# Four weight loads issued on ScalarE's queue, ahead of its table load, in a linear-attention and MLP block

## The chip, the cores and the metric

The kernel runs on one NeuronCore of a Trainium2 chip. The metric is the device time of one execution in microseconds, as the median of the runs; the median of a changed kernel is compared with the median of the kernel before. A profile (one execution recorded by the hardware profiler) gives the rest: its times count from the start of its span.

In the profile's rows PE is TensorE (PEld its weight loads), DVE is VectorE, ACT is ScalarE, POOL is GpSimd, and SP is SyncE, which only issues DMAs. A "q" behind an engine means its sequencer. `L361` is line 361 of the kernel.

## The reference

A block of two parallel branches over 2048 tokens of width 512, all in float32: a layer norm without weights, a linear attention of 32 heads with 16 columns each, and a two-layer MLP with a squared ReLU and 1376 hidden columns.

```python
def reference(A_x, A_wqkv, A_wo, B_x, B_w1, B_b1, B_w2, B_b2):
    def _A_ref(x, wqkv, wo):
        B, S, D = x.shape
        H = 32; Dh = D // H
        qkv = (lambda x, *d: x.transpose(*d))((x @ wqkv).reshape(B, S, 3, H, Dh), 2, 0, 3, 1, 4)
        q, k, v = qkv[0], qkv[1], qkv[2]
        phi = lambda t: jnp.where(t > 0, t + 1, jnp.exp(t)) + 1e-6
        pq, pk = phi(q), phi(k)
        kv = jnp.einsum("bhsd,bhse->bhde", pk, v)
        z = jnp.einsum("bhsd->bhd", pk)
        num = jnp.einsum("bhqd,bhde->bhqe", pq, kv)
        den = jnp.einsum("bhqd,bhd->bhq", pq, z)[..., None] + 1e-6
        o = num / den
        return (lambda x, *d: x.transpose(*d))(o, 0, 2, 1, 3).reshape(B, S, D) @ wo
...
    x = A_x
    xn = _layernorm(x, axis=-1)
    return x + _A_ref(xn, A_wqkv, A_wo) + _B_ref(xn, B_w1, B_b1, B_w2, B_b2)
```

## The kernel before

The 2048 tokens are 16 tiles of 128 rows (`NT = 16`, `P = 128`). A float32 product is made from float32r parts: each operand is split into a high part and the rest, and three of the four partial products are added in PSUM (`wk[0]`, `wk[1]` are the high and low part of the key weights, `xsb` those of the transposed tokens). The kernel first runs over the 16 token tiles for the keys and the sums that linear attention needs (`kx`), then over queries, attention and the MLP. The order of instructions on each engine is the order in which the code writes them (`manual_schedule`); the framework adds the semaphore waits.

What matters here is the start, before the first product.

- ScalarE loads its function table in the first lines of the kernel (L68); its first ACTIVATE is the logarithm for tile 0's inverse root (L225).
- TensorE runs 11 matmuls on zeros (L472), which appear as 22 rows in the profile, while the first data comes.
- SyncE issues, one after the other on its queue: token tile 0 and token tile 1 (`x0`, 256 KB each, `load_x`, L156), the four chunks of the key columns of `wqkv` (`rk`, `load_k`, L479: 128 rows of 2 KB each, cut out of rows of 6 KB), token tiles 2 and 3 in one load (`x2`, 512 KB, L156), and, behind a wait for a small copy on GpSimd (L540), token tiles 4 to 7 (`x4`, 1 MB). Only SyncE issues DMAs in the whole kernel.
- VectorE takes the statistics of tile 0, then of tile 1 (L214 and L215; each waits for its tile's load). Then come three short steps that refine the inverse root of tile 0 (L234 to L236), its normalisation (`xp`, L253), and the same for tile 1.
- ScalarE, behind the logarithm and exponential of tile 0 and of tile 1 (L225, L226), copies the high part of key chunk 0 (`wkh<-rk`, L109, in `heads_k`), then the transposed tokens of tile 0 (`xs1h`, L316), then chunk 1, and so on; chunks 2 and 3 come later.
- TensorE transposes tile 0 (`pt`, L300) when it is normalised, and begins the key products (`pk`, L361) with the first half of tile 0 and key chunk 0.

Of the kernel before, what the change touches and what calls it, by code (L numbers as in the profile page):

```python
# [18 lines left out]
def kernel(  # L19
# [29 lines left out]
    nc = tc.nc  # L49
    xf = x.rearrange("b s d -> (b s) d")  # L50
    of = out.rearrange("b s d -> (b s) d")
    S, D = xf.shape
# [11 lines left out]
    FP = NF * P  # L64
    FL = F - (NF - 1) * P
    assert D == 512 and S % BT == 0 and FL % 32 == 0 and FL < P

    nc.scalar.preload_act_table_set("natural_log_exp_and_others")  # L68

    keep = ctx.enter_context(tc.tile_pool(name="keep", bufs=1))  # L70
    work = ctx.enter_context(tc.tile_pool(name="work", bufs=1))
# [12 lines left out]
    def next_tag(of):  # L84
        k, n = turns[of]
        turns[of][0] = (k + 1) % n
        return f"{of}{k}"

    def two(name):
        return keep.tile([P, 2, 512], F32, name=name, tag=next_tag("x"))  # L90

    def four(name, tag, dt=F32, pool=None):
        return (pool or work).tile([P, TB, 512], dt, name=name, tag=tag)
# [60 lines left out]
    def load_x(i, t):  # L154
        n = t.shape[1]
        nc.sync.dma_start(t, xf[i * P:(i + n) * P, :].rearrange("(i p) d -> p i d", i=n))  # L156
        for k in range(n):
            xr[i + k] = t[:, k]
# [6 lines left out]
    def chunk(w, j, a, b):  # L165

        return w[j * P:(j + 1) * P, a:b]
# [306 lines left out]
    t, rk = two("x0"), four("rk", "r0")  # L474
    for i in range(2):
        load_x(i, t[:, i:i + 1])
    def load_k(*js):
        for j in js:
            nc.sync.dma_start(rk[:, j], chunk(wqkv, j, D, 2 * D))  # L479

    load_k(*range(NJ))
    load_x(2, two("x2"))
    nc.gpsimd.memset(ident, 0.0)
    nc.gpsimd.affine_select(out=ident, in_=ident, compare_op=OP.not_equal, fill=1.0, base=0,
# [629 lines left out]
```

## Time and profile before

| | |
|---|---|
| median of 3 runs | 422.36 us (422.19 to 422.56) |
| the profiled execution | 422.49 us, of which the span is 420.8 us |
| PE busy | 415.2 us (99%) |
| PE weight loads busy | 343.6 us (82%) |
| DVE / ACT / POOL busy | 294.2 / 254.0 / 27.6 us |
| granted TensorE clock | 1.00 |
| DMA | 46.16 MB, mean 110 GB/s |
| first transpose on PE (L300) | starts at 6.46 us |

A row of the timeline gives the start, the length, the engine, the line and the operation, and in brackets how long the engine was idle before it and what ended that. The chain of waits is followed back from the last instruction to what released each step; it tells which work set the end. A row of the stages gives a window and its length, then for each engine its busy time and the number of its instructions, and last the granted clock, the mean share of the 16 DMA engines that is busy, and GB/s. A DMA row ends with the time from issue to landing.

### The profile page before, as it was taken

How to read it: one execution, taken by the hardware profiler on the slowest of the kernel's cores; microseconds unless marked ns; L12 is line 12 of the kernel's file. 1: busy time of each engine (PE TensorE's matmuls, PEld its weight loads, DVE VectorE, ACT ScalarE, POOL GpSimd, SP SyncE). 2: the span in 40 equal slices, each digit the busy share in tenths (PEclk: the TensorE clock that was granted, in tenths of full speed). 3: DMA queues.
4: the chain of work that ended last, by engine and by line, in shares of the span. 5: the costliest groups of instructions: out<-in, count | busy, mean ns of one | idle time of the engine just before them, and what ended most of it. 6: DMA issues, size and time to landing. Idle time of an engine off the chain costs nothing.

```text
span 420.8 us, 5373 instructions
## 1 busy us (share of the span) xinstructions
PE 415.2 (99%) x1860; PEld 343.6 (82%) x1860; DVE 294.2 (70%) x536; ACT 254.0 (60%) x451; POOL 27.6 (7%) x50
## 2 busy tenths in 40 slices
PE   7999999999999999999999999999999999999996
PEld 7788888888887888888888888888888888888885
DVE  6886767777578877677579475586967667577343
ACT  5867777675467767665457362676667665546230
POOL 3242222220000000000000000000000000000000
PEclk9999999999999999999999999999999999999999
DMA  7885422800412231645026652401120654024502
GB/s 240 286 243 157 130 89 92 278 15 3 112 50 77 75 100 26 199 82 169 0 85 191 173 196 97 124 0 50 51 75 25 202 101 149 2 95 97 152 0 100
DMA packets 44818, 46.16 MB, mean 110 GB/s; under 512 B 5716, under 2 KB 31060, under 8 KB 44536
## 3 DMA queue, kind: packets, MB, share of 16 engines
q1 hardware_dynamic: 44792, 45.84, 36.5%
q8 instruction: 14, 0.23, 0.2%
q14 instruction: 12, 0.10, 0.1%
HBM read 32.71 MB, written 8.91 MB: 99 GB/s over the span
## 4 chain that ended last, share of the span: by engine, by line
PE 98%; DVE 1%; DMA 1%; ACT 0%; issue 0%
PE acc L128 39%; PE b L453 23%; PE kx L380 10%; PE pk L361 10%; PE pq L361 10%; PE pz L128 1%; PE b L128 1%; PE pkv L773 1%; PE pm L128 1%; DMA x<-in_A_x_dram 1%; PE pt L300 1%; PE end L128 0%; DVE st L214 0%; DVE xp L253 0%; DVE res L903 0%; ACT xs1h L316 0%
## 5 line engine op out<-in xcount | busy, mean ns | idle before, releaser
L128 PE MATMUL acc<-w2r,s 128*128 128x512 f32 x498 | 116.6, 389 | 0.0
L128 PEld LDWEIGHTS acc<-w2r,s 128*128 128x128 f32 x498 | 93.5, 188 | 19.6
L453 PE MATMUL b<-T,aop 128*128 128x512 f32 x240 | 59.6, 389 | 0.0
L453 PEld LDWEIGHTS b<-T,aop 128*128 128x128 f32 x240 | 45.0, 188 | 9.4
L380 PE MATMUL kx<-pk,tok 128*128 128x512 f32 x192 | 46.8, 392 | 0.0
L380 PEld LDWEIGHTS kx<-pk,tok 128*128 128x128 f32 x192 | 35.6, 188 | 7.9 <-DVE pk L369 0.6
L128 PE MATMUL acc<-mh,aTsr 128*128 128x512 f32 x96 | 30.3, 390 | 0.0
L109 ACT ACTIVATE w2r<-r 128x512 fp32r<-128x512 f32 x32 | 20.0, 625 | 13.8 <-PE acc L128 11.3
L120 DVE TENSOR_TENSOR w2r<-r,w2r 128x512 fp32r<-128x512 f32 x32 | 21.9, 685 | 7.3 <-ACT w2r L109 7.2
L453 PE MATMUL b<-xs0h,aop 128*128 128x512 f32 x80 | 26.4, 391 | 0.0
L117 POOL TENSOR_TENSOR tok<-xp,tok 128x512 fp32r<-128x512 f32 x16 | 21.7, 1362 | 54.9 <-ACT tok L109 54.9
L117 DVE TENSOR_TENSOR s<-c,s 128x512 fp32r<-128x512 f32 x20 | 13.8, 692 | 16.3 <-ACT s L109 16.3
L356 DVE SCALAR_TENSOR_TENSOR q<-pq,q 128x512 f32<-128x512 f32 x16 | 11.0, 689 | 14.9 <-ACT q L354 14.9
L109 ACT ACTIVATE aop<-S 128x512 fp32r<-128x512 f32 x20 | 12.6, 629 | 14.6 <-DVE S L702 9.4
L128 PEld LDWEIGHTS acc<-mh,aTsr 128*128 128x128 f32 x96 | 18.0, 188 | 3.8
L903 DVE TENSOR_TENSOR res<-acc,res 128x512 f32<-128x512 f32 x16 | 11.0, 692 | 14.2 <-PE acc L128 14.2
L352 ACT ACTIVATE q<-pq 128x512 f32<-128x512 f32 x16 | 9.4, 591 | 18.5 <-PE pq L361 18.5
L199 POOL MEMSET r<- 32x512 f32 x3 | 1.6, 522 | 278.2 <-DVE w2r L120 272.3
L128 PE MATMUL acc<-ml,aTsr 128*128 128x512 f32 x48 | 18.7, 390 | 0.0
L453 PEld LDWEIGHTS b<-xs0h,aop 128*128 128x128 f32 x80 | 15.0, 188 | 3.4 <-ACT rz L441 0.3
L453 PE MATMUL b<-xs0l,aop 128*128 128x512 f32 x40 | 15.6, 389 | 0.0
L285 DVE STREAM_TRANSPOSE at<-g 128x512 f32<-128x512 f32 x16 | 10.5, 689 | 6.8 <-DMA g<-q 6.8
(192 smaller groups left out, 826.7 us busy)
## 6 DMA issues: line engine op xcount, KB each, us to landing
r<-in_B_w_dram SPq DMA_DIRECT2D x49, 256.0 KB, 3.2
res<-in_A_x_dram SPq DMA_DIRECT2D x8, 512.0 KB, 5.9
g<-q SPq DMA_DIRECT2D x64, 64.0 KB, 2.1
out_dram<-res SPq DMA_DIRECT2D x15, 256.0 KB, 2.1
x<-in_A_x_dram SPq DMA_DIRECT2D x5, 512.0 KB, 5.6
via<-xp SPq DMA_DIRECT2D x5, 512.0 KB, 2.6
xg<-via SPq DMA_DIRECT2D x20, 128.0 KB, 3.0
xTd<-t SPq DMA_DIRECT2D x8, 256.0 KB, 3.1
```

The costliest lines, as they stand in the source:

```text
L109: nc.scalar.activation(o, i, AF.Copy, bias=bias)
L117: ENG[el].tensor_tensor(out=l, in0=src, in1=f32(h), op=OP.subtract)
L120: nc.vector.tensor_tensor(out=l, in0=src, in1=f32(h), op=OP.subtract)
L128: nc.tensor.matmul(ps, lhsT=a[u], rhs=b[v], start=first and n == 0, stop=last and n == 2)
L285: nc.vector.transpose(o.rearrange("p j (r t) -> p r j t", r=NJ), G.rearrange("p r (j c) -> p r j c", j=NJ))
L300: nc.tensor.transpose(t[k][:, at:at + P], xp[i][:, j * P:(j + 1) * P], ident)
L352: nc.scalar.activation(p, ps, AF.Relu, scale=-1.0)
L356: nc.vector.scalar_tensor_tensor(p, ps, 0.0, p, op0=OP.max, op1=OP.add)
L361: nc.tensor.matmul(ps, lhsT=cols(i)[u][:, j, slot(i)], rhs=w[v][:, j, :], start=first and n == 0, stop=last and n == len(steps) - 1)
L380: nc.tensor.matmul(kxp[c], lhsT=tok[i][:, u, c * P:(c + 1) * P], rhs=pk[i][:, v], start=i == 0 and (u, v) == first, stop=i == NT - 1 and ( ...
L453: nc.tensor.matmul(ps, lhsT=a[u][:, j * P:(j + 1) * P], rhs=b[v][:, j, :], start=first and j == 0 and n == 0, stop=last and j == 1 and n == 2,
L903: nc.vector.tensor_tensor(out=r[:, a:z], in0=ps, in1=r[:, a:z], op=OP.add)
```

## The change

The table load moves from the head of the kernel to behind the four loads of the key chunks, and these four are issued by ScalarE in place of SyncE. On ScalarE the order is then: four DMA issues, the table load, and all else as before. On SyncE it is: tile 0, tile 1, tiles 2 and 3, and all else as before. The instructions of the other engines and their order are the same. As two lines fall away and one comes in, a line of the kernel after stands one or two numbers lower than in the kernel before (L214 becomes L212, L484 becomes L483).

```diff
@@ -65,8 +65,6 @@
     FL = F - (NF - 1) * P
     assert D == 512 and S % BT == 0 and FL % 32 == 0 and FL < P
 
-    nc.scalar.preload_act_table_set("natural_log_exp_and_others")
-
     keep = ctx.enter_context(tc.tile_pool(name="keep", bufs=1))
     work = ctx.enter_context(tc.tile_pool(name="work", bufs=1))
     small = ctx.enter_context(tc.tile_pool(name="small", bufs=4))
@@ -476,9 +474,10 @@
         load_x(i, t[:, i:i + 1])
     def load_k(*js):
         for j in js:
-            nc.sync.dma_start(rk[:, j], chunk(wqkv, j, D, 2 * D))
+            nc.scalar.dma_start(rk[:, j], chunk(wqkv, j, D, 2 * D))
 
     load_k(*range(NJ))
+    nc.scalar.preload_act_table_set("natural_log_exp_and_others")
     load_x(2, two("x2"))
     nc.gpsimd.memset(ident, 0.0)
     nc.gpsimd.affine_select(out=ident, in_=ident, compare_op=OP.not_equal, fill=1.0, base=0,
```

## The prediction

> **What bounds the kernel now.** I read the chain of waits first, over the first 30 us. Its columns are start, length (us) and what held the end.
>
> ```profile
> 0.82 2.76 DMA x<-in_A_x_dram
> ...
> 3.60 0.71 DVE st L214
> ...
> 4.51 0.59 DVE st L214
> ...
> 5.77 0.55 DVE xp L253
> ...
> 6.46 0.42 PE pt L300 x2
> ...
> 6.91 0.39 ACT xs1h L316
> ...
> 7.35 0.50 PE pk L361
> 7.85 0.44 PE pt L300 x4
> 8.28 4.34 PE pk L361 x19
> ```
>
> The reader is to see that the chain enters TensorE at 6.46 and never leaves it again: 19 matmuls in 4.34 us are 0.228 us each, and line 4 of the page gives PE 98% of the whole span. So nothing after about 8 us can be gained or hidden; what moves the first transpose (L300) moves the end by as much. Ahead of it stands one DMA, the load of token tile 0, and then VectorE's own order: statistics of tile 0, statistics of tile 1, and only then the normalisation of tile 0 (L234 to L253). So tile 1's landing is on this path too, as soon as it comes after VectorE is ready for it.
>
> The timeline (start, length, engine, line, operation) gives the issues and who is ready when.
>
> ```profile
> 0.81 1.28 ACT L68 ACT_TABLE_LOAD   x1 [0.81 <-PEq L1100]
> 0.82 0.86 SPq L156 DMA_DIRECT2D x<-in_A_x_dram  x2
> ...
> 1.72 1.85 SPq L479 DMA_DIRECT2D rk<-in_A_wqkv_dram  x4
> ...
> 3.62 4.23 SPq L156 DMA_DIRECT2D x<-in_A_x_dram  x2
> ...
> 4.43 0.66 DVE L214 BATCH_NORM_STATS2 st<-x 128x6 f32<-128x512 f32 x1
> 4.55 0.29 ACT L225 ACTIVATE y<-mv,eps 128x1 f32<-128x1 f32 x1 [2.45 <-DVE mv L215]
> ```
>
> Tile 1's statistics start at 4.43 with no wait in brackets: x1 had landed, by how much earlier this view doesn't say. The table load ends at 2.09, 2.46 us before ScalarE's first ACTIVATE.
>
> Then the transfers: issue to landing of the key chunks one by one (last number), and the DMA engines by stage (last three columns: clock, DMA share, GB/s).
>
> ```profile
> rk<-in_A_wqkv_dram SPq DMA_DIRECT2D x1, 256.0 KB, 4.1
> ...
> rk<-in_A_wqkv_dram SPq DMA_DIRECT2D x1, 256.0 KB, 4.3
> ```
>
> ```profile
> 1.85:2.50 0.65, 0.65 (x5) 0.65 (x5) 0.00 (x0) 0.24 (x1) 0.52 (x4) 1.00 0.94 189
> 2.50:3.10 0.60, 0.60 (x4) 0.60 (x4) 0.00 (x0) 0.00 (x0) 0.04 (x1) 1.00 0.99 328
> 3.10:3.60 0.50, 0.50 (x5) 0.50 (x4) 0.00 (x1) 0.00 (x0) 0.00 (x0) 1.00 1.06 397
> 3.60:4.20 0.60, 0.60 (x5) 0.60 (x5) 0.60 (x1) 0.00 (x0) 0.00 (x0) 1.00 0.91 242
> 4.20:4.80 0.60, 0.60 (x5) 0.60 (x5) 0.56 (x3) 0.25 (x1) 0.00 (x0) 1.00 0.66 249
> 4.80:5.40 0.60, 0.55 (x5) 0.35 (x4) 0.53 (x4) 0.30 (x3) 0.00 (x0) 1.00 1.13 318
> 5.40:6.00 0.60, 0.00 (x0) 0.00 (x0) 0.53 (x3) 0.57 (x3) 0.00 (x0) 1.00 0.99 341
> ```
>
> From 1.85 to 3.6 the 16 DMA engines are full (0.94 to 1.06) while they carry x0 and x1 alone. Length times GB/s adds up to 123, 320, 518, 663, 812, 1003 and 1208 thousand bytes at the ends of these rows. One 256 KB load is 262 thousand: x0 has moved at 2.92, x0 and x1 together at 3.62, a third load at 4.69, a fourth at 5.53. x0 landed at 3.58, 0.66 after its bytes. The key chunks 0 and 1, third and fourth, landed at 1.72 + 4.1 = 5.82 and about 2.19 + 4.3 = 6.49 (issues 0.47 apart).
>
> **The change part by part.** *Table load behind four issues.* ScalarE now starts with four DMA issues. On SyncE the same four take 1.85 us together; so the table load runs from about 2.66 to 3.95, still 0.60 before the 4.55 at which ScalarE is first wanted: cost 0. Bounds: an issue may cost between 0.43 and the longest single issue near here, 1.20 (the one of L652). From 0.61 each the cover by tile 0's load and statistics is gone and every microsecond counts; but if tile 1 is late, as below, VectorE first wants y0 behind tile 1's statistics, and the issues may then take about 1.0 each. I take 0.43.
>
> *SyncE without the four.* It is free 1.90 us sooner, so x2 (512 KB) is issued at about 1.72 instead of 3.62. The load of x4 behind it waits for GpSimd's copy (L540, at 7.26), which waits for tile 1's normalisation constants, so it moves with the path; the stores and loads behind it follow. x2 landed at about 9.1 and its statistics begin at 9.52 behind other VectorE work: sooner is worth 0.
>
> *Key chunks sooner.* wkh of chunk 0 (5.81) stands on ScalarE behind the roots of tile 1, done at 5.87 by the timeline's rows, so its landing at 5.82 held nothing: 0 gained. At most the three wider gaps between matmul starts from 6.8 to 8.4 (0.53, 0.34, 0.31 instead of 0.23) could shrink, 0.5 us in all, and the rows put these to the transposes and to xs1h, not to the keys. Chunks 2 and 3 are wanted at 8.91; x2 and they together end where the same 2.1 MB ended before, about 9.1, and with the path 1.4 later that is hidden by 1.2 us. Without that delay it would cost 0.2.
>
> *Token tiles share the engines.* This is the term that counts. Before, x0 and x1 had full engines for themselves. Now rk0 starts at 0.81 on ScalarE's queue beside x0 at 0.82, and rk1 beside x1. If the engines serve both queues evenly, x0 ends with 524 thousand bytes moved and x1 with 1049 thousand, twice as far down. Ends for x1's landing: at the best rate of the rows (397 GB/s) from 1.85 with the ramp of the first row (0.65 us for 123 thousand), 2.50 + 926/397 = 4.83, plus x0's 0.66 = 5.49; or as rk1 did with as many bytes ahead, 6.49. I take 5.8, under the middle, since the idle third of the engines in 4.20 to 4.80 (0.34 x 0.6 = 0.2 us) gets work sooner. Tile 1's statistics then start 0.02 behind the landing, at 5.82 instead of 4.43: +1.4. x0's own delay (landing about 4.3 instead of 3.58) is inside that: its statistics end before x1 comes. From there every row up to 6.46 follows in its old order, and TensorE passes all of it on.
>
> The Trainium skill, page "DMA: Bandwidth & Descriptors", section "Issuing engines are not separate DMA queues", speaks against this change: DMAs issued from the scalar and sync engines run on the same 16 engines and interleave, and a second issuer saves only issue time. The full DMA share beside x0 agrees; by this rule the sum is a loss, not a gain.
>
> *Sum:* 0 + 0 + 0 + 1.4. The profiled execution took 422.49 (span 420.8 and 1.7 around it) and would take 423.9, with a span of 422.2. It is 0.13 above the median of 422.36; against that median the sum is 422.36 + 1.4 = **423.8**.
>
> **The rivals.** *B, whole loads in turn:* each engine serves one queue's share of a whole load, then the other's: x0, rk0, x1, rk1. Then x1 is the third, landing between 4.69 (bytes alone) and 5.82 (as rk0 did); 4.69 + 0.66 = 5.35 is +0.94: 423.3. For it: x0's share on one engine is only 262/16 = 16 thousand bytes. Against it: ScalarE may be first, and then x1 is fourth again. The same page, section "Queues, rings and completion order", says that an engine drains a packet of some 9 to 17 descriptors from one row before it turns to the next; nothing in this trace has two busy load queues, so no row agrees or disagrees.
>
> *C, not slower:* the mechanism is a head start of SyncE's loads, its place the DMA engines' queues at 1.85. If x0 and x1 are served before the keys (ScalarE's queue starts later, or is served behind), x1 lands before 4.43 and nothing changes: 422.4. It decides when ScalarE's first bytes come over about 1 us after SyncE's. Against it: both issuers are released within 0.01 us.
>
> *D, faster:* the gaps of 0.5 us from 6.8 to 8.4 and the ramp of the first row (189 GB/s against 397, 0.3 us) both vanish because two queues fill the engines sooner: -0.8, 421.5. Against it: the share is 0.94 already in the ramp.
>
> *E, clock drop:* between the warm-up matmuls (end 5.34) and L300 (6.46) TensorE idles 1.12; with +1.4 it is 2.5. The warm-up starts 18 matmuls in its first 3.77 us, 0.21 each, and 6 rows lie in its last 0.72, 0.12 each: the same work at half and at full pace. If the idle stretch brings the slow pace back for as long, half of 3.77 is lost: +1.9, 425.7. The Trainium skill, "TensorE: Matmul & The Clock Gate", Part 1, has the clock fall only after an idle window of about 3.4 us; by it 2.5 is safe, and no run here shows where the limit lies.
>
> *F, the table load ends last:* with issues of 1.20 each on ScalarE it ends at 0.81 + 4.8 + 1.28 = 6.89; the roots of tile 0 then end 0.5 later, at 7.4, against the 6.7 at which VectorE would want them: +0.7 more, 424.5.
>
> **How the numbers follow.** The likeliest case 0.50, B 0.20, C 0.14, D 0.04, E 0.06, F 0.06. I call no change what lies within 0.2%, 0.84 us, about what a measurement here can tell from none. Slower: 0.50, E and F 0.12, and 0.11 of B (its low end is below +0.84): 0.73. Same: C and the rest of B, 0.23. Faster: 0.04. Range: the likeliest's own is 423.4 to 424.5 (5.49 and 6.49); down to C's 422.3, up to 424.9 so that part of E stays out.
>
> **What would show it.** After: x1's landing at 5.5 to 6.5, an idle DVE before the second L212 (its L214) put to DMA x, the first transpose at about 7.9, the matmuls behind it at 0.228 as before, a table load that ends near 3.95. B shows as x1 near 5.3. C would show the second statistics still at 4.43, and the sum fails. E would show matmuls at 0.4 us start to start behind the transposes; F an idle DVE put to ACT y.

## The result, and the profile after

The changed kernel takes 425.18 us (median of 6 executions, 424.83 to 426.15), the kernel before 422.52 beside it (422.19 to 422.76). The ratio is 1.0066, with a 95% interval of 1.0053 to 1.0079: 2.7 us slower. The profiled execution is the longest of the six, 426.15 with a span of 424.4, 3.6 us more than the span before.

The chain of waits after (start, length, what held the end):

```profile
1.26 4.18 DMA x<-in_A_x_dram
...
5.46 0.70 DVE st L212
...
7.54 0.67 PE pt L298 x2
...
8.67 0.79 PE pk L359
9.46 0.85 PE pt L298 x4
10.31 5.94 PE pk L359 x19
```

The DMA at the head is now the second token tile's, issued at 1.26. The second statistics start at 5.46 instead of 4.43, 1.03 late, and the first transposes at 7.54 instead of 6.46, 1.08 late. Then the same work takes longer on TensorE itself: from the first transpose to the 19 matmuls 10.31 - 7.54 = 2.77 instead of 1.82, and the 19 matmuls 5.94 instead of 4.34, 0.313 each on average instead of 0.228. 1.08 + 0.95 + 1.60 = 3.63, the whole difference of the two spans.

The start in the timeline (the length of a row that joins several issues runs from the first to the end of the last, so the 8.56 of SyncE's row is mostly waiting), and the loads one by one with their time to landing:

```profile
0.81 1.87 ACTq L477 DMA_DIRECT2D rk<-in_A_wqkv_dram  x4
...
0.81 8.56 SPq L154 DMA_DIRECT2D x<-in_A_x_dram  x4
...
2.71 1.28 ACT L480 ACT_TABLE_LOAD   x1 [2.71 <-issue]
4.48 0.69 DVE L212 BATCH_NORM_STATS2 st<-x 128x6 f32<-128x512 f32 x1 [3.54 <-DMA x<-in_A_x_dram]
...
5.46 0.69 DVE L212 BATCH_NORM_STATS2 st<-x 128x6 f32<-128x512 f32 x1
```

```profile
rk<-in_A_wqkv_dram ACTq DMA_DIRECT2D x1, 256.0 KB, 3.8
...
rk<-in_A_wqkv_dram ACTq DMA_DIRECT2D x1, 256.0 KB, 4.6
x<-in_A_x_dram SPq DMA_DIRECT2D x1, 256.0 KB, 4.2
```

Key chunk 0 lands at 0.81 + 3.8 = 4.6, and tile 0 just before 4.48; tile 1 at 1.26 + 4.2 = 5.5, key chunk 1 at about 1.25 + 4.6 = 5.85. The loads come in pairs, one of each queue. The table load ends at 2.71 + 1.28 = 3.99, well before ScalarE's first ACTIVATE at 5.42.

The granted clock is the share of full speed at which TensorE is let run. Here are stretches of 3.41 us, which is how long the half-speed stretches on record last (window, length, PE busy and the number of matmuls that lie in it wholly or in part, clock, DMA share, GB/s):

```profile
3.33:6.74 3.41, 2.56 (x12) 1.00 1.01 377
6.74:10.16 3.42, 2.58 (x10) 1.00 0.32 120
10.16:13.57 3.41, 3.41 (x10) 1.00 0.79 302
13.57:16.90 3.33, 3.33 (x18) 1.00 0.62 157
```

A stretch that is full of matmuls holds 10 of them up to 13.57, and 18 behind it. The clock column says 1.00 throughout, because the trace has no clock record before the first grant of full speed; the pace tells that TensorE ran at half speed until 13.57. (The mean granted clock of this execution, 0.999, comes from the last 1.3 us of the span, behind the last matmul, where the clock is 0.50.) The other five executions have a mean granted clock of 0.996 over spans of 423.1 to 423.5: 0.004 x 423.4 / 0.5 = 3.4 us at half speed, which by this estimate costs 1.7. With the 1.03 by which the second statistics are late that is 2.7, the median's loss.

### The profile page after: what moved, and what is told of

Read it like the earlier page. It is cut to its first block, busy times and chain, and to the rows that moved or that the text cites. A ratio compares the mean times of both kernels' runs of the same rounds, so it can differ in the third digit from the quotient of the medians.

```text
span 424.4 us, 5374 instructions
## 1 busy us (share of the span) xinstructions
PE 418.6 (99%) x1860; PEld 346.1 (82%) x1860; DVE 294.5 (69%) x536; ACT 253.9 (60%) x451; POOL 27.6 (7%) x50
## 4 chain that ended last, share of the span: by engine, by line
PE 97%; DMA 1%; DVE 1%; issue 0%; ACT 0%; SPq 0%
PE acc L126 38%; PE b L451 22%; PE pk L359 11%; PE kx L378 10%; PE pq L359 10%; PE pz L126 1%; PE b L126 1%; DMA x<-in_A_x_dram 1%; PE pkv L772 1%; PE pt L298 1%; PE pm L126 1%; PE end L126 0%; DVE st L212 0%; DVE xp L251 0%; DVE res L902 0%
```

## The experiments

Each was timed beside the kernel before, which took 422.48 to 422.56. Lines of the kernels stand within two or so of those above.

**The kernel after with a longer warm-up.**

```diff
-    WARM = 11
+    WARM = 16
```

> The kernel after, with 16 warm-up matmuls (32 rows) instead of 11 (22 rows), so that TensorE has work until about 7 us. Theory 1: of the +2.7 us, 1.0 is tile 1's late landing (second statistics at 5.46 instead of 4.43) and the rest a slow TensorE clock that follows the longer idle stretch ahead of the first transpose; without that stretch the time is 422.5 + 1.0 = 423.5, and no matmul behind the first transposes is 0.4 us after the one before. Theory 2: the rest is late data further on (key chunks, tiles 2 and 3, later loads); then more warm-up work changes nothing and the time stays at 425.2.

423.75, ratio 1.0033 (1.0022 to 1.0045). The second statistics are as late as in the kernel after, at 5.54, but the loss is 1.2 instead of 2.7. In its profile TensorE's stretches are:

```profile
2.17:5.58 3.41, 3.41 (x18) 1.00 0.97 347
5.58:8.99 3.41, 2.46 (x19) 1.00 0.70 260
```

and in its timeline the first transposes start at

```profile
7.62 0.63 PE L298 MATMUL pt<-ident,xp 128*128 128x128 f32 x4 [0.70 <-DVE y L232]
```

The first stretch is full of warm-up rows, the next is still busy for 2.46, and behind it the matmuls follow at 0.23. The first transposes are 1.16 late (7.62 instead of 6.46), and that is about the whole of the 1.2. Theory 1 holds, theory 2 falls: no data further on was late.

**The kernel before with the longer warm-up** (the same edit).

> The kernel before, with 16 warm-up matmuls instead of 11. Control: both theories expect 422.5, if the added 10 rows end before the first transpose is ready at 6.46 us; at the slow pace of 0.21 us a row all 32 would end at 7.7 and cost up to 1.2, at the fast pace from 4.6 on they end at 6.2 and cost nothing.

422.76, ratio 1.0007 (0.9998 to 1.0016): no difference that the interval can tell. By itself the longer warm-up makes the kernel no faster, and by the interval at most 0.7 slower.

**The delay without the transfers.** In the kernel before, between the two statistics:

```diff
-    two_tiles = statistics(0), statistics(1)
+    two_tiles = [statistics(0)]
+    for _ in range(2):
+        nc.vector.tensor_scalar(zb, xr[0], two_tiles[0][2][:, 0, 0:1], two_tiles[0][2][:, 0, 1:2], op0=OP.subtract, op1=OP.mult)
+    two_tiles.append(statistics(1))
```

> The kernel before, its transfers unchanged, with two more VectorE instructions of the normalisation's form (0.55 us each) between the statistics of tile 0 and of tile 1; their result is overwritten later and not used. The first transpose is thereby 1.1 us late, with no change to any DMA. Theory 1: a late start of any cause lets the clock fall: 422.5 + 1.1 + 1.7 = 425.3. Theory 2 (the rest of the loss comes from the DMAs): 422.5 + 1.1 = 423.6, and the matmuls keep the fast pace.

425.29, ratio 1.0056 (1.0038 to 1.0073): nearly the whole loss of the kernel after, with every DMA as before. The executions lie at 423.8 (two of six, granted clock 1.00), 425.2 to 425.4 (three, 0.995 to 0.996) and 426.5 (one, 0.991). The profiled one is one of the first kind:

```profile
2.99:6.40 3.41, 2.90 (x14) 1.00 0.92 293
6.40:9.81 3.41, 1.99 (x12) 1.00 0.67 242
```

```profile
7.57 0.63 PE L300 MATMUL pt<-ident,xp 128*128 128x128 f32 x4 [1.68 <-DVE y L234]
```

The first transposes are 1.11 late here, and these two executions lose little more than that. With 1.99 of 3.41 busy the clock stayed.

> before_late (two more VectorE instructions, whose result is not used, between the two statistics; no DMA changed) with 16 warm-up matmuls instead of 11. Theory 1 (the idle stretch ahead of the first transpose makes the clock fall): the late start alone stays, 422.5 + 1.1 = 423.6 to 423.8, and few or no executions above 425. If the late start cost 2.7 by some other way than the clock, it stays at 425.3.

With `WARM = 16` on top, 424.02, ratio 1.0033 (1.0023 to 1.0043), 0.2 above what was expected: the late start remains, most of the clock's share is gone. None of its 12 executions has a granted clock below 0.998. One lies above 425, the profiled one at 425.24: its clock stays at 1.00, and TensorE waits 1.0 us much later, for VectorE (`aTsr`, L120), as it does for 1.1 us in the profile of before_warm16 (424.02), so that wait has nothing to do with the start.

**Half the delay**: `range(1)` in place of `range(2)`.

> The kernel before with one more VectorE instruction of 0.55 us between the two statistics (its result is not used), half the dose of before_late. TensorE then idles about 1.7 us ahead of the first transpose instead of 1.1. If the clock falls only for a longer idle stretch: 422.5 + 0.55 = 423.1 in all executions. If the limit lies nearer: a mixture of 423.1 and some 424.7, the loss of one slow stretch on top.

424.46, ratio 1.0039 (1.0024 to 1.0054), and all six executions between 424.3 and 424.8. Five have a granted clock of 0.994 to 0.996; the sixth, the profiled one, was late with the first grant. So 0.55 us of delay costs 1.9: 423.1 was met by no execution, and all of them lie near the upper value of the mixture. The kernel before stands closer to the edge than either expectation had it; one of its own 66 executions beside these runs took 424.16 at a granted clock of 0.996. Whether the shorter delay loses the clock more often than the longer one (four of six) six executions can't tell.

**The keys on ScalarE, behind the table load.** L68 is left where it was; only the issuing engine in `load_k` is changed.

> The key loads on ScalarE's queue, but behind the table load, which stays at the head of the kernel: the first key chunk is then issued at about 2.1 us, 0.4 later than before, and tiles 0 and 1 have the DMA engines alone as before. Theory 1: tile 1 is on time (second statistics at 4.43), the clock is kept, 422.5; key chunk 0 lands at about 6.2 instead of 5.8, which moves its copy on ScalarE to 6.2 and still ends before the transposed tokens are wanted at 6.91. Theory 2 (a second DMA queue in itself costs): slower than 423.5.

425.13, ratio 1.0059 (1.0040 to 1.0078): as slow as the kernel after. Theory 1's number failed, for a reason that the timeline shows:

```profile
0.81 1.28 ACT L68 ACT_TABLE_LOAD   x1 [0.81 <-PEq L1100]
0.81 8.02 SPq L156 DMA_DIRECT2D x<-in_A_x_dram  x4
0.84 1.84 ACTq L479 DMA_DIRECT2D rk<-in_A_wqkv_dram  x4
```

ScalarE's sequencer issues the DMAs while the engine loads its table. The key loads start at 0.84, 0.03 later than in the kernel after, so this run gave the tokens no head start and could not test it. It does show that the table load's place decides nothing. Its stretches show a loss of the clock in full:

```profile
1.82:5.23 3.41, 3.41 (x18) 1.00 0.94 339
5.23:8.65 3.42, 1.35 (x9) 1.00 0.73 276
8.65:12.06 3.41, 3.41 (x11) 0.50 0.65 219
12.06:15.47 3.41, 3.41 (x19) 1.00 0.65 203
```

A stretch that is busy for 1.35 of 3.42 is followed by one at a granted clock of 0.50, which holds 11 matmuls where the next full one holds 19.

**A real head start.** In the kernel after, the keys wait for GpSimd's mask:

```diff
-    load_k(*range(NJ))
-    nc.scalar.preload_act_table_set("natural_log_exp_and_others")
     load_x(2, two("x2"))
...
+    nc.scalar.preload_act_table_set("natural_log_exp_and_others")
+    nc.scalar.activation(zb[:, :1], heads[:, :1], AF.Copy)
+    load_k(*range(NJ))
     nc.gpsimd.memset(b1s[:, NF - 1:], 0.0)
```

> The kernel after, with the four key loads on ScalarE held back by one small copy that waits for GpSimd's mask (done at about 2.4 us; the copy's result is not used); the table load is ahead of it. Same queues, same loads, but tiles 0 and 1 have a head start of 1.1 to 1.6 us. Theory 1 (tile 1 is late because the key chunks share the engines with it): second statistics back at about 4.4, clock kept, 422.5, though key chunk 0 now shares the engines with tiles 2 and 3 and lands at 5.5 to 6.2, still in time. Theory 2 (a second load queue or ScalarE's issues as such cost): 423.5 or more.

423.63, ratio 1.0033 (1.0013 to 1.0053); the executions range from 422.63 to 426.72, and the profiled one is the longest of the twelve. The tokens are on time, the second statistics at 4.52 and the first transposes at 6.56, but now a key chunk is late:

```profile
4.52 0.66 DVE L212 BATCH_NORM_STATS2 st<-x 128x6 f32<-128x512 f32 x1
...
7.79 0.63 ACT L107 ACTIVATE wkh<-rk 128x512 fp32r<-128x512 f32 x1 [1.83 <-DMA rk<-in_A_wqkv_dram]
```

Chunk 0, issued at 2.39, lands 5.4 later, at 7.8, where 5.5 to 6.2 had been expected. SyncE now issues the 512 KB of tiles 2 and 3 ahead of it, and the expectation that the two share the engines from the start fails: the trace has the first packet of ScalarE's queue at 5.39, 3.0 behind its issue, where in the kernel after it came 1.2 behind (2.02 for 0.81). Until 5.39 only SyncE's queue moved data. Why ScalarE's waited is open. So the time didn't separate the theories, though the timeline clears the tokens.

**The same, with tiles 2 and 3 behind the keys.**

```diff
     load_k(*range(NJ))
+    load_x(2, two("x2"), nc.scalar)
...
-    load_x(2, two("x2"))
```

> keys_held with tiles 2 and 3 also on ScalarE's queue, behind the four keys; SyncE issues tiles 0 and 1 alone. Held back as there by a copy whose result is not used. If keys_held's late key chunk 0 (copied at 7.8) came from sharing with tiles 2 and 3, chunk 0 now has the engines to itself once tile 1 is in and lands at 5.3 to 6.2, and the time is that of the kernel before, 422.5 to 422.8. If the ScalarE queue is slow as such, chunk 0 is late again and the time stays at 423.6.

422.82, ratio 1.0012 (1.0000 to 1.0023): of the loss 0.3 is left, and the interval reaches down to none, with the four keys still on ScalarE's queue and two queues in use. Two of the 12 executions still lose the clock (424.31 and 424.53, both at 0.996). The first packet of ScalarE's queue comes at 3.99, when the 0.52 MB of tiles 0 and 1 have moved: the tokens had the engines to themselves. Chunk 0 takes 3.6 and is copied at 6.05:

```profile
4.41 0.66 DVE L212 BATCH_NORM_STATS2 st<-x 128x6 f32<-128x512 f32 x1
...
6.05 0.63 ACT L107 ACTIVATE wkh<-rk 128x512 fp32r<-128x512 f32 x1 [0.20 <-DMA rk<-in_A_wqkv_dram]
```

**One key chunk instead of four.** In the kernel before:

```diff
-            nc.sync.dma_start(rk[:, j], chunk(wqkv, j, D, 2 * D))
+            (nc.scalar if j == NJ - 1 else nc.sync).dma_start(rk[:, j], chunk(wqkv, j, D, 2 * D))
```

> The kernel before, with only the last of the four key loads (chunk 3) on ScalarE's queue, behind the table load at the head; chunks 0 to 2 stay on SyncE. Theory 1 (both queues are served evenly from the first bytes, so any one load beside tile 0 makes it late): first statistics at about 4.4 as in the kernel after instead of 3.6, the second right behind at about 5.3, the first transpose 0.8 to 0.9 late, and the slow clock on top in most executions: 424.3 to 425.2. Theory 2 (the delay goes with the number of bytes moved over): a quarter of the kernel after's delay, 0.26, too little for the clock to fall often: 422.8.

425.12, ratio 1.0053 (1.0037 to 1.0069): a quarter of the change costs as much as all of it.

```profile
4.67 0.69 DVE L214 BATCH_NORM_STATS2 st<-x 128x6 f32<-128x512 f32 x1 [3.73 <-DMA x<-in_A_x_dram]
...
5.50 0.68 DVE L214 BATCH_NORM_STATS2 st<-x 128x6 f32<-128x512 f32 x1
```

Tile 0 alone is late by 1.07 here; the second statistics follow at VectorE's own pace, with no wait.

**Both queues for the tokens alone.** In the kernel before, tiles 0 and 1 in two halves of 64 rows each:

```diff
-        load_x(i, t[:, i:i + 1])
+        for e, a in ((nc.sync, 0), (nc.scalar, 64)):
+            e.dma_start(t[a:a + 64, i], xf[i * P + a:i * P + a + 64, :])
+        xr[i] = t[:, i]
```

> The kernel before, with tiles 0 and 1 each loaded in two halves of 64 rows, one from SyncE and one from ScalarE (behind the table load); the keys stay on SyncE. Two queues carry nothing but the first tokens. If issue and ramp limit the first load (189 GB/s in its first 0.65 us against 397 later), tile 0 lands 0.1 to 0.3 sooner: 422.2 to 422.4. If only the engines' rate counts: 422.5. If half loads cost more at their start: up to 423.

426.11, ratio 1.0077 (1.0061 to 1.0093), worse than anything expected.

```profile
0.81 1.22 SPq L477 DMA_DIRECT2D x<-in_A_x_dram  x2
0.84 1.47 ACTq L477 DMA_DIRECT2D x<-in_A_x_dram  x2
...
6.62 0.69 DVE L214 BATCH_NORM_STATS2 st<-x 128x6 f32<-128x512 f32 x1 [1.59 <-DMA x<-in_A_x_dram]
```

Two half loads take 1.22 and 1.47 to issue, where two whole ones take 0.86, and the last half of tile 1 comes at 6.6. That it then shares the engines with key chunk 0, as SyncE goes on to it, fits but wasn't tested. The first transposes start at 8.69, 2.2 late, and a stretch at a granted clock of 0.50 follows (9.11 to 12.52).

## Why the prediction was wrong

*What bounds the kernel:* the path is right. Whatever moved the first transpose moved the end; before_late shows it without a DMA. That the end moves "by as much" failed: there 1.1 of delay cost 2.7 (see E).

*The table load behind four issues, cost 0:* right. The issues took 1.87, the table load ran from 2.71 to 3.99 (2.66 to 3.95 predicted). Rival F is refuted; table_first shows in addition that a table load ahead of the issues would not have held them up.

*SyncE without the four, and the keys sooner, 0 each:* right. Key chunk 0's copy starts at 6.84, behind the second root, as before. In after_warm16 the late start, 1.16 us, is about the whole loss of 1.2, which leaves nothing for these two.

*The tokens share the engines:* the mechanism is right, the size was 1.4 and measured 1.03. Both queues are served evenly: had whole loads gone in turn (B), tile 0 or key chunk 0 would have come a load's 0.6 us ahead of the other, near 3.6 to 4.0; they came at 4.5 and 4.6, and up to 3.60 the two queues had taken 28.4% and 28.7% of the engines' time. B's +0.94 is nearer to 1.03 than 1.4 is, but by luck, as its order of loads is not the trace's. The head start of C decides as it said, but wasn't there: keys_held_x2 gives it, and all but 0.3 of the loss is gone. The term was too large because the rates before, 242 to 249 GB/s from 3.60 to 4.80, had been carried over in part. In the kernel after they are gone:

```profile
3.60:4.20 0.60, 0.60 (x5) 0.60 (x5) 0.00 (x0) 0.40 (x1) 0.00 (x0) 1.00 1.06 410
4.20:4.80 0.60, 0.60 (x4) 0.60 (x4) 0.32 (x1) 0.00 (x0) 0.00 (x0) 1.00 1.04 399
```

Length times rate, added up from 1.85 over all rows, puts the first four loads in at 4.93 instead of 5.53. The working also took tile 0's delay as hidden in tile 1's. It is the larger part: 4.48 - 3.60 = 0.88, and only 0.15 more comes from tile 1. That is why one_key costs as much.

*E, the clock:* this is the step that failed. The sum let TensorE pass the delay on one for one, with matmuls "at 0.228 as before", and so put the clock at 0. The clock stood as a rival with a chance of 0.06, when it comes on top of the likeliest case and in nearly every execution: 1.0 + 1.7 = 2.7. Its price of 1.9 was near (of the six rows in the warm-up's last 0.72 us two had begun before, but the four others start 0.11 apart, so the two paces were read rightly); its 425.7 is 0.5 too high mainly because it carries the 1.4. Its mechanism, a slow pace that comes back, fits the five executions at 0.996; in the profiled one the slow pace had not yet ended.

The chance was put low by the idle time in one piece, 2.5 us at most. What the stretches show instead fits a decision on the busy share of each fixed 3.41 us: the clock stayed after 1.99 (before_late), 2.46 (after_warm16) and, in the kernel before,

```profile
4.62:8.03 3.41, 2.03 (x15) 1.00 1.02 357
```

after 2.03; it fell after 1.35 (table_first), with no idle piece over 1.81. Other stretches of these runs narrow it, some of them at the end of the kernel: it stayed after 1.78 (before_warm16, 417.23 to 420.64) and 1.80 (table_first, 418.25 to 421.66), and fell after 1.41 (keys_held), 1.48 (one_key, 5.80 to 9.21) and 1.52 (keys_held_x2, 416.22 to 419.63). So the kernel before, at 2.03, was 0.25 to 0.5 us of work away from a fall already. The Trainium skill, "TensorE: Matmul & The Clock Gate", Part 1, has the clock fall after an idle window of about 3.4 us; the length of the stretches agrees, 3.41, but a window need not be idle to count, and here the measurement decides. after_warm16 keeps the data late and brings back 1.4 of the 2.7; before_late takes the data's part away and keeps the loss. So the split of the 2.7 is shown from both sides.

*D, faster:* the ramp did not vanish (224 GB/s from 1.85 to 2.50, 189 before), and the gaps remained: in after_warm16, at full clock, the matmuls from 8.50 on start 0.34, 0.35 and 0.32 apart.

The experiments gave no version faster than the kernel before; keys_held_x2 is the nearest with ScalarE's queue in use.

## What to carry to other kernels

Loads that are issued at once on two queues share the DMA engines from their first bytes. Here that moved the bytes of four loads sooner (4.93 instead of 5.53), but the two token tiles were needed first and came later (statistics at 4.48 and 5.46 instead of 3.60 and 4.43). So the load that everything waits for should have a head start, 1.6 us here (keys_held_x2), and one load beside it does as much harm as four. A delay ahead of the first matmuls costs more than itself where a warm-up holds TensorE's clock: the warm-up should leave little idle time ahead of the first real work, and where one load can come late, be longer than needed (16 matmuls instead of 11 took back 1.4 of the 2.7 here). Price such a delay as the delay plus half of one slow stretch, not as an unlikely rival.

## What the runs showed of the hardware

- The clock changes in stretches of 3.41 us, whose position differs between executions (the first grant lay at 4.62, 5.23, 5.58, 6.40 and 13.57). Once granted, it was kept at 1.78 of 3.41 busy and more, and lost at 1.52 and less; where between these values the limit lies is open. For the first grant more was needed, but the busy time alone doesn't settle it: it came after 2.67 (keys_held_x2, 3.21 to 6.62) and 2.90 (before_late), and not after 2.56 and 2.58 (the kernel after) or 2.77 (before_late1, 0.21 to 3.62). The ends of matmuls, and so the busy times, are modelled. At half speed the same work also takes about twice as long (warm-up rows start 0.21 apart instead of 0.11), so the two limits compare as times, not as work.
- After one stretch at 0.50 the clock came back when that stretch was full (table_first). In the profile of keys_held it was not:

```profile
4.49:7.90 3.41, 1.41 (x11) 1.00 0.99 351
7.90:11.32 3.42, 2.58 (x8) 0.50 0.82 270
11.32:14.73 3.41, 3.41 (x9) 0.50 0.35 130
```

  There 2.58 of 3.42 did not suffice, and a second stretch at half speed followed; that execution took 426.72.
- A DMA issued from ScalarE doesn't wait for a table load ahead of it (issue at 0.84, table load from 0.81 to 2.09).
- Two loads of 64 rows (128 KB) took longer to issue than two of 128 rows: 1.22 and 1.47 against 0.86. That the rows are the reason isn't shown: the first key load behind them on SyncE, with 128 rows, took 0.59 too, and the next ones 0.43.
- In the kernel before, with one queue, the DMA engines were at a share of 0.66 and 249 GB/s between 4.20 and 4.80; in the kernel after, with two, at 1.04 and 399. It isn't a rule of two queues: tokens_split, with half loads on both, had 0.76 and 201 there. Why is open.
- A load issued while the other queue is busy can wait instead of sharing: in keys_held the first packet of ScalarE's queue came 3.0 us behind its issue, in keys_held_x2 1.6, in the kernel after 1.2.
